# A last block stored from fp32, a last load in halves, and two gate pairs in one row-tiled session: a fused attention and gated-FFN kernel on one core

## Chip, cores and metric

The kernel runs on one core of one Trainium2 chip. The metric is the device time in microseconds. Before the change it was 753.76 us, the median of 6 runs (749.32 to 759.1).

## What is computed

x has 4 batches of 12416 tokens with 128 channels; 32 inducing points I (32x128) are shared by the batches. Two attention steps make new tokens, and a gated FFN of width 1536 follows:

```python
h    = softmax(I @ x.T / sqrt(128)) @ x        # per batch: 32 x 128
y    = softmax(x @ h.T / sqrt(128)) @ h        # per batch: 12416 x 128
gate = sigmoid(y @ w_gate)
out  = (gate * (y @ w_val)) @ w_out            # 49664 x 128, fp32
```

Since y is a mixture of the 32 rows of h, the kernel never forms it: y @ w_gate is the 32-column attention matrix times h @ w_gate. The sigmoid is half of (1 + tanh(half the argument)); the half is applied when the output is evicted.

## The kernel before, in words

**Tiles.** 12288 tokens of a batch are six "quads" of 2048 (QT), and 128 tokens are left as a tail. A block is 512 tokens; 96 blocks cover the quads, and the last one, number 96, is "mixed": the four tails of 128 tokens together. The 1536 columns of the FFN are 12 chunks j of 128. A gate pair p is the chunks 2p and 2p+1.

**Head (lines 81 to 569).** GpSimd issues the six loads of batch 0's quads (`load_x`, L83, with a cast to fp16) and then the loads of the three weights (L116 to L120). For each quad s, TensorE transposes it in two halves of eight 128x128 tiles (`xT_pe`, L476; ScalarE copies half 0 out of PSUM, VectorE half 1), computes 16 scores (`s1n`, L506, with an exp on ScalarE), and accumulates h (`h_mm`, L193). The loop of L515 staggers them: scores of quad s-1, transposes of s, h of s-2. Then h is normalised, multiplied with the weights (`hw_mm`, L242), and `hw_pad` (L256) has GpSimd copy some chunks of it into `pads`, tiles of 128 rows that are zero elsewhere.

**Fills (L351).** The 32 rows of h @ w for a chunk lie in one of four row groups of 32: gates in groups 0 and 1, values in 2 and 3; `rep` holds the attention matrix four times, once for each group. A fill is one matmul of 512 columns with the 32 rows of one group (a row-tiled fill), or, for chunks that have a padded copy (PADG, PADV, L133), with all 128 rows. Before the change PADG is (2, 5): gate pairs 2 and 5 are filled with 128 rows. PADV is (2, 5, 8, 11): one value chunk in each step.

**Main loop (L718).** Each block has four steps k. A step, in program order:

1. `v_fill` of two value chunks into the PSUM tile va (one buffer, two banks), row-tiled
2. one gate pair into a tile g (two buffers of two banks), then its tanh on ScalarE (`g_tanh`, L418, writing T)
3. `v_mul` (L432): VectorE makes u = (T + 1) * va
4. c0 output matmuls (`out_mm`, L445) from the queue `ready`
5. `v_fill` of one value chunk into vb (one buffer, one bank), 128 rows
6. at odd k one more gate pair; at k = 2, in 49 of the blocks, a job (`do_extra`, L651: scores, h sums and the like for a later batch or quad)
7. `v_mul` of vb; c1 output matmuls

Items 1 and 2 are the step's row-tiled session. Gates run ahead of the values: at k = 0 pair 3 is filled, at k = 1 pairs 4 (in the session) and 5 (after vb, 128 rows), at k = 2 pair 0 of the next block, at k = 3 its pairs 1 (in the session) and 2 (after vb, 128 rows). (c0, c1) come from PLAN (L712), or PLAN_JOB where the block has a job. All engines run in the order written (`manual_schedule`, L78); each engine's queue is in order.

**Outputs.** A block's 12 output matmuls accumulate [channels x 512 tokens] in the tile acc (one buffer, one bank). `out_store` (L456) then has ScalarE evict it with the factor 0.5 to fp16 (oT), SP issue a DMA transpose to `on` (tokens on partitions), and GpSimd issue the store, which casts to fp32. For the mixed block these are four stores, one for each batch (L473).

Of the kernel before, what the change touches and what calls it, by code (L numbers as in the profile page):

```python
# [9 lines left out]
F32 = mybir.dt.float32  # L10
F16 = mybir.dt.float16
# [5 lines left out]
P = 128  # L17
TOK = 512
QT = 4 * TOK
# [4 lines left out]
def kernel(  # L24
# [41 lines left out]
    def slot_g(name):  # L66
        return ps_g.tile([P, 2 * TOK], F32, tag="g", name=name)
# [15 lines left out]
    def load_x(b, q):  # L83
        t = xqp.tile([P, QT], F16, tag="xq", name=f"xq_{b}_{q}")
        nc.gpsimd.dma_start(  # L85
            t[:], x[b, ds(q * QT, QT)].rearrange("(p j) c -> p (j c)", j=QT // P)
        )
        xqs[(b, q)] = t
# [24 lines left out]
        out=ident[:], in_=ident[:], compare_op=ALU.not_equal, fill=1.0, base=0,  # L113
        pattern=[[-1, P]], channel_multiplier=1,
    )
    for q in range(2, NQ):  # L116
        load_x(0, q)
    nc.gpsimd.dma_start(wg16[:], moe_w_gate.rearrange("c (j f) -> c j f", f=P))
    nc.gpsimd.dma_start(wv16[:], moe_w_val.rearrange("c (j f) -> c j f", f=P))
    nc.gpsimd.dma_start(wo16[:], moe_w_out.rearrange("(j p) c -> p j c", p=P))  # L120
# [9 lines left out]
    hTs = [pers.tile([P, M], F16, tag=f"hT{b}", name=f"hT_{b}") for b in range(B)]  # L130
    hws = [pers.tile([P, NP2, P], F16, tag=f"hw{b}", name=f"hw_{b}") for b in range(B)]

    PADG, PADV = (2, 5), (2, 5, 8, 11)  # L133
    pads = [pers.tile([P, 8, P], F16, tag=f"hwp{b}", name=f"hwp_{b}") for b in range(B)]
    for t_ in pads:
        nc.gpsimd.memset(t_[:], 0.0)

# [38 lines left out]
    def s1n_mm(ps, b, q, lo, hi):  # L176
        for tk in range(lo, hi):
            j, r = tk % 4, tk // 4
            nc.tensor.matmul(
                ps[:, ds((j * 4 + r) * M, M)], xTs[b][:, ds(q * QT + tk * P, P)], indT[:],  # L180
                start=True, stop=True,
            )
# [10 lines left out]
    def h_mm(ps, b, q, first, last, tail, ch=0, cs=P):  # L193
        for j in range(4):
            nc.tensor.matmul(  # L195
                ps[:, cs:cs + P], ones[:, 0:P], a1n[(b, q)][:, j, :],
                start=first and j == 0, stop=last and j == 3,
            )
            if tail and j == 0:
                nc.tensor.matmul(  # L200
                    ps[:, cs:cs + M], ones[:, 0:P], a1n[(b, "t")][:], start=False, stop=False
                )
        for j in range(4):
            for r in range(4):
                nc.tensor.matmul(  # L205
                    ps[r * M:(r + 1) * M, ch:ch + P],
                    a1_chunk(b, q, 4 * r + j),
                    xqs[(b, q)][:, ts(4 * r + j, P)],
                    start=first and j == 0,
                    stop=last and j == 3 and not (tail and r == 0),  # L210
                )
        if tail:
            nc.tensor.matmul(
                ps[0:M, ch:ch + P], a1n[(b, "t")][:], xtail[:, b, :], start=False, stop=last,
            )
# [40 lines left out]
    def hw_pad(b):  # L256
        for i, p in enumerate(PADG):
            for jj in range(2):
                rows = slice(jj * M, (jj + 1) * M)
                nc.gpsimd.tensor_copy(out=pads[b][rows, 2 * i + jj, :], in_=hws[b][rows, p, :])  # L260
        for i, j in enumerate(PADV):
            g = 2 + j % 2
            rows = slice(g * M, (g + 1) * M)
            nc.gpsimd.tensor_copy(out=pads[b][rows, 4 + i, :], in_=hws[b][rows, j // 2, :])

# [80 lines left out]
    blocks.append(dict(T=B * P, mixed=True))  # L348
    NBK = len(blocks)

    def fill(ps, col, bi, j, val):  # L351
        k = blocks[bi]
        g = (j % 2) + (2 if val else 0)
        if val and j in PADV:
            pad = 4 + PADV.index(j)
        elif not val and j // 2 in PADG:
            pad = 2 * PADG.index(j // 2) + j % 2
        else:
            pad = None
        rows = slice(0, P) if pad is not None else slice(g * M, (g + 1) * M)  # L360

        def weights(b):
            return pads[b][:, pad, :] if pad is not None else hws[b][rows, j // 2, :]

        if not k["mixed"]:
            rep = reps[(k["b"], k["d"])]
            nc.tensor.matmul(  # L367
                ps[:, ds(col, TOK)], weights(k["b"]), rep[rows, 4 * k["i"] + k["r"]],
                start=True, stop=True,
            )  # L370
        else:
            rep = reps["m"]
            for b in range(B):
                nc.tensor.matmul(
                    ps[:, ds(col + b * P, P)], weights(b), rep[rows, b, :],
                    start=True, stop=True,
                )
# [31 lines left out]

    Ts = {}  # L410

    def g_fill(bi, p):
        ps = slot_g(f"g_{bi}_{p}")
        for jj in range(2):
            fill(ps, jj * TOK, bi, 2 * p + jj, False)
        return ps

    def g_tanh(bi, p, ps):  # L418
# [25 lines left out]

    def out_mm(bi, j, u):  # L445
        T = blocks[bi]["T"]
        if bi not in accs:
            accs[bi] = slot_o(f"acc_{bi}")
            done_out[bi] = 0
        c = done_out[bi]  # L450
        nc.tensor.matmul(  # L451
            accs[bi][:, 0:T], wo16[:, j, :], u, start=(c == 0), stop=(c == NJ - 1)
        )
        done_out[bi] = c + 1

    def out_store(bi):  # L456
        k = blocks[bi]
        T = k["T"]
        nch = T // P
        oT = outp.tile([P, TOK], F16, tag="oT", name=f"oT_{bi}")  # L460
        nc.scalar.activation(out=oT[:, 0:T], in_=accs[bi][:, 0:T], func=AF.Copy, scale=0.5)  # L461
        on = outp.tile([P, 4, C], F16, tag="on", name=f"on_{bi}")
        nc.sync.dma_start(on[:, 0:nch, :], oT[:, 0:T], transpose=True)
        if not k["mixed"]:
            row0 = k["b"] * N + (2 * k["d"] + k["i"]) * QT
            nc.gpsimd.dma_start(  # L466
                out[ds(row0, QT)].rearrange("(p j) c -> p j c", j=QT // P)[
                    :, 4 * k["r"]:4 * k["r"] + 4, :],
                on[:],
            )  # L470
        else:
            for b in range(B):
                nc.gpsimd.dma_start(out[ds(b * N + NT0, P)], on[:, b, :])  # L473


    def xT_pe(b, q):  # L476
        for half in range(2):
            ps = slot_g(f"xt_{b}_{q}_{half}")
            v = ps[:].bitcast(F16)
            for j in range(8):  # L480
                nc.tensor.transpose(  # L481
                    v[:, ts(j, P)], xqs[(b, q)][:, ts(8 * half + j, P)], ident[:]
                )
            dst = xTs[b][:, ds(q * QT + half * 8 * P, 8 * P)]
            if half:
                nc.vector.tensor_copy(out=dst, in_=v[:, 0:8 * P])  # L486
            else:
                nc.scalar.copy(out=dst, in_=v[:, 0:8 * P])

    ps = slot_a("warm")  # L490
    warm(ps, 16)
# [11 lines left out]
    s1t_exp(0, ps)  # L503

    hps = slot_a("h_0")
    def s1n(q):  # L506
        an = ep.tile([P, 4, P], F16, tag="a1q", bufs=3, name=f"a1q_0_{q}")
        ps = (slot_o if q % 2 else slot_b)(f"s1n_0_{q}")
        s1n_mm(ps, 0, q, 0, 16)
        nc.scalar.activation(  # L510
            out=an[:].rearrange("p j f -> p (j f)"), in_=ps[:, 0:TOK], func=AF.Exp, scale=SCALE,
        )
        a1n[(0, q)] = an

    for s in range(NQ):  # L515
        if s >= 1:
            s1n(s - 1)
        xT_pe(0, s)
        if s >= 2:
            h_mm(hps, 0, s - 2, s == 2, False, s == 2, TOK, 0)  # L520
    s1n(NQ - 1)
    h_mm(hps, 0, NQ - 2, False, False, False, TOK, 0)
    h_mm(hps, 0, NQ - 1, False, True, False, TOK, 0)
    psd = slot_g("warm2")
    warm(psd, 1)
# [165 lines left out]
    gdone = 0  # L691
    gwant = LEADP

    def g_next():
        nonlocal gdone
        bi, p = divmod(gdone, NP2)
        gp = g_fill(bi, p)
        g_tanh(bi, p, gp)
        gdone += 1

# [8 lines left out]

    PLAN = ((2, 3), (1, 2), (1, 2), (1, 2))  # L712
    PLAN_JOB = ((2, 3), (1, 2), (1, 1), (1, 2))

    g_next()
    g_next()
# [1 line left out]
    for n in range(NBK):  # L718
        for k in range(4):
            for f in ev.get((n, k), ()):  # L720
                f()
            c0, c1 = (PLAN_JOB if n in extra else PLAN)[k]
            gwant = min(NG, gwant + 1)
            ps = slot_a(f"va_{n}_{k}")
            v_fill(ps, n, 3 * k, 2)
            if gdone < gwant:
                g_next()
            ua = v_mul(ps, n, 3 * k, 2)
            ready.extend(prev)
            outs(c0)  # L730
            ps = slot_b(f"vb_{n}_{k}")
            v_fill(ps, n, 3 * k + 2, 1)
            if k % 2:
                gwant = min(NG, gwant + 1)
            post = None
            if k == 2 and n in extra:
                post = do_extra(*extra[n])
            elif gdone < gwant:
                g_next()
            ub = v_mul(ps, n, 3 * k + 2, 1)  # L740
            if post:
                post()
            outs(c1)
            prev = ua + ub
# [34 lines left out]
```

## Time and profile before

| what | value |
|---|---|
| median of 6 runs | 753.76 us |
| profiled execution, its own time | 750.49 us |
| its span | 748.7 us |
| granted TensorE clock, mean | 0.993 |
| ACT T<-g, 582 tanhs of 128x1024 | 568.6 us busy, mean 1023 ns |
| DVE u<-T,va, 388 of 128x1024 | 472.9 us busy, mean 1219 ns |
| DVE u<-T,vb, 388 of 128x512 | 263.6 us busy, mean 679 ns |
| PE acc<-u,wo, 1164 matmuls | 380.9 us busy, mean 382 ns |
| PE g<-rep,hwp, 384 matmuls (128 rows) | 113.8 us busy, mean 377 ns |
| PE g<-rep,hw, 768 matmuls (32 rows) | 148.8 us busy, mean 384 ns |
| wait PE va <- DVE u | 51.3 us, 154 times |
| wait ACT T <- PE g | 49.1 us, 84 times |

A row of the profile's groups reads: line, engine, operation, out<-in, shapes, count; then busy time and the mean of one; then the idle time of the engine just before. A row of the timeline reads: start, duration, engine, line, operation, count, and in brackets how long the engine had idled and what released it. PE is the matmul, PEld the weight load. A matmul's duration is its latency: two of 512 columns on the same rows start about 0.21 us apart, though each shows 0.38. SPq, POOLq are the queues of those engines.

### The profile page before, as it was taken

The numbers are of one execution on the slowest core, as the hardware profiler recorded it, in microseconds if no ns is written. First come the engines' busy times: TensorE is split into PE (matmuls) and PEld (weight loads), VectorE is DVE, ScalarE is ACT, GpSimd is POOL, SyncE is SP. The second block draws the span as 40 slices with busy tenths as digits, with TensorE's granted clock in tenths as the row PEclk, the third lists the DMA queues.
The fourth block names the chain that finished last, engine by engine and source line by source line (L and its number), as shares of the span: only waits on it lengthen the run. The fifth ranks groups of instructions, "written<-read, shape, count | busy, mean of one in ns | idle before, by whom it ended". The sixth has DMA issues, their size and how long they took to land.

```text
span 748.7 us, 12241 instructions
## 1 busy us (share of the span) xinstructions
PE 667.0 (89%) x4525; PEld 250.0 (33%) x4525; DVE 708.3 (95%) x838; ACT 652.5 (87%) x725; POOL 215.0 (29%) x328
## 2 busy tenths in 40 slices
PE   7888999989889889989889899999888888888884
PEld 4433333333333333333333333333333333333332
DVE  2599999999999999999999999999999999999994
ACT  4699999899899989889989989989989989989883
POOL 5236214304413412402611601521530430330001
PEclk9999999999999999999999999999999999999998
DMA  9578994523558997523347899442352352252222
GB/s 179 81 108 151 214 190 96 113 49 72 106 94 157 145 177 155 115 57 78 80 99 139 118 200 180 102 89 56 69 115 51 71 120 57 70 108 60 59 49 57
DMA packets 182300, 80.25 MB, mean 107 GB/s; under 512 B 165952, under 2 KB 166624, under 8 KB 182240
## 3 DMA queue, kind: packets, MB, share of 16 engines
q1 hardware_dynamic: 162112, 40.18, 31.8%
q0 software_dynamic: 20128, 39.30, 24.5%
q8 instruction: 35, 0.57, 0.3%
q14 instruction: 25, 0.20, 0.1%
HBM read 27.80 MB, written 25.43 MB: 71 GB/s over the span
## 4 chain that ended last, share of the span: by engine, by line
DVE 33%; PE 32%; ACT 24%; DMA 6%; issue 3%; POOL 1%; SPq 0%; POOLq 0%; DVEq 0%; ACTq 0%
DVE u L435 31%; ACT T L422 17%; PE acc L451 12%; PE va L367 9%; PE g L367 6%; ACT oT L461 3%; PE vb L367 3%; DMA xT<-xq 3%; DMA xq<-in_x_dram 2%; ACT e L281 1%; ACT e L164 1%; DMA on<-oT 1%; DVE hacc L221 1%; PE h L205 1%; PE h L195 0%
## 5 line engine op out<-in xcount | busy, mean ns | idle before, releaser
L422 ACT ACTIVATE T<-g 128x1024 f16<-128x1024 f32 x582 | 568.6, 1023 | 61.3 <-PE g L367 49.1
L435 DVE SCALAR_TENSOR_TENSOR u<-T,va 128x1024 f16<-128x1024 f16 x388 | 472.9, 1219 | 8.8 <-issue 3.6
L451 PE MATMUL acc<-u,wo 128*128 128x512 f16 x1164 | 380.9, 382 | 5.3 <-DVE u L435 0.4
L435 DVE SCALAR_TENSOR_TENSOR u<-T,vb 128x512 f16<-128x512 f16 x388 | 263.6, 679 | 0.0
L367 PE MATMUL va<-rep,hw 32*128 32x512 f16 x768 | 149.5, 381 | 54.1 <-DVE u L435 51.3
L466 POOL DMA_DIRECT2D out_dram<-on x96 | 52.8, 550 | 478.4 <-DMA on<-oT 469.5
L451 PEld LDWEIGHTS <-wo 128*128 128x128 f16 x1164 | 104.6, 97 | 173.3 <-issue 99.0
L367 PE MATMUL g<-rep,hw 32*128 32x512 f16 x768 | 148.8, 384 | 0.3 <-ACT T L422 0.2
L367 PE MATMUL vb<-rep,hwp 128*128 128x512 f16 x384 | 144.9, 377 | 0.0
L367 PEld LDWEIGHTS <-hw 32*128 32x128 f16 x1536 | 55.5, 91 | 205.1 <-issue 202.5
L367 PE MATMUL g<-rep,hwp 128*128 128x512 f16 x384 | 113.8, 377 | 2.7 <-DVE hT L240 1.8
L367 PEld LDWEIGHTS <-hwp 128*128 128x128 f16 x768 | 74.2, 97 | 71.5 <-issue 25.1
L321 POOL TENSOR_TENSOR a<-e2n,rc 128x512 f16<-128x512 f16 x88 | 89.3, 1042 | 6.1 <-DVE rc L311 5.8
L461 ACT ACTIVATE oT<-acc 128x512 f16<-128x512 f32 x97 | 58.5, 603 | 6.7 <-PE acc L451 3.9
L303 POOL TENSOR_TENSOR tree<-tree 128x256 f32<-128x256 f32 (+2 forms) x33 | 16.2, 491 | 2.6
L303 POOL TENSOR_TENSOR tree<-e2n 128x512 f32<-128x512 f16 x11 | 12.6, 1148 | 11.5 <-DMA e2n<-e 11.5
L486 DVE COPY xT<-xt 128x1024 f16<-128x1024 f16 x6 | 4.2, 692 | 11.6 <-PE xt L481 11.6
L85 POOL DMA_DIRECT2D xq<-in_x_dram x24 | 13.6, 568 | 0.8 <-POOLq L763 0.8
L164 ACT ACTIVATE e<-s 128x1024 f16<-128x1024 f32 x9 | 9.2, 1024 | 3.9 <-PE s L656 3.9
L281 ACT ACTIVATE e<-s 128x1024 f16<-128x1024 f32 x11 | 11.3, 1024 | 0.0
L656 PE MATMUL s<-xT,indT 128*32 128x512 f16 x72 | 6.3, 386 | 3.5 <-DMA xT<-xq 3.5
L260 POOL COPY hwp<-hw 32x128 f16<-32x128 f16 x16 | 4.6, 289 | 16.0 <-ACT hw L253 15.4
(89 smaller groups left out, 159.7 us busy)
## 6 DMA issues: line engine op xcount, KB each, us to landing
out_dram<-on POOLq DMA_DIRECT2D x96, 256.0 KB, 2.7
xq<-in_x_dram POOLq DMA_DIRECT2D x24, 512.0 KB, 6.3
on<-oT SPq DMA_TRANSPOSE x97, 2.4
wg<-in_moe_w_gate_dram POOLq DMA_DIRECT2D x1, 384.0 KB, 16.4
wv<-in_moe_w_val_dram POOLq DMA_DIRECT2D x1, 384.0 KB, 17.8
wo<-in_moe_w_out_dram POOLq DMA_DIRECT2D x1, 384.0 KB, 18.8
rep<-a SPq DMA_TRANSPOSE x22, 4.3
xT<-xq SPq DMA_TRANSPOSE x18, 5.4
```

The costliest lines, as they stand in the source:

```text
L85: nc.gpsimd.dma_start(t[:], x[b, ds(q * QT, QT)].rearrange("(p j) c -> p (j c)", j=QT // P))
L164: nc.scalar.activation(out=e1[:, 0:w], in_=ps[:, 0:w], func=AF.Exp, scale=SCALE)
L205: nc.tensor.matmul(ps[r * M:(r + 1) * M, ch:ch + P], a1_chunk(b, q, 4 * r + j), xqs[(b, q)][:, ts(4 * r + j, P)], start=first and j == 0, ...
L281: nc.scalar.activation(out=e2[:], in_=ps[:], func=AF.Exp, scale=SCALE)
L303: nc.gpsimd.tensor_tensor(out=nxt, in0=cur[:, :, 0:w], in1=cur[:, :, w:2 * w], op=ALU.add)
L321: nc.gpsimd.tensor_tensor(out=a2[:, r], in0=e2n[:, i, :, r, :].unsqueeze(2).to_broadcast((P, 4, 4, M)), in1=rc[:, i, :, r].unsqueeze(2).un ...
L367: nc.tensor.matmul(ps[:, ds(col, TOK)], weights(k["b"]), rep[rows, 4 * k["i"] + k["r"]], start=True, stop=True,)
L422: nc.scalar.activation(out=Ts[bi][:, 2 * p:2 * p + 2, 0:T], in_=ps[:].rearrange("p (a t) -> p a t", a=2)[:, :, 0:T], func=AF.Tanh, scale=0.5,)
L435: nc.vector.scalar_tensor_tensor(out=u[:, :, 0:T], in0=Ts[bi][:, j0:j0 + n, 0:T], scalar=1.0, in1=ps[:].rearrange("p (a t) -> p a t", t=TO ...
L451: nc.tensor.matmul(accs[bi][:, 0:T], wo16[:, j, :], u, start=(c == 0), stop=(c == NJ - 1))
L461: nc.scalar.activation(out=oT[:, 0:T], in_=accs[bi][:, 0:T], func=AF.Copy, scale=0.5)
L466: nc.gpsimd.dma_start(out[ds(row0, QT)].rearrange("(p j) c -> p j c", j=QT // P)[:, 4 * k["r"]:4 * k["r"] + 4, :], on[:],)
```

## The change

- Batch 0's last quad is loaded by two DMAs of 8 tokens a partition each; its transposes, scores and exps are done in halves. In the loop's last turn h of quad 3 stands between the transposes of half 0 and half 1; scores of half 0, h of quad 4, scores of half 1, h of quad 5 follow. With halves, `s1n` writes its exp with a four-dimensional pattern.
- PADG is (2,). Pair 5 is always row-tiled. Pair 2 uses its padded weights only where it is filled after vb (`whole`, at k = 3). `pads` shrinks from 8 to 6 chunks, and `hw_pad` copies two chunks fewer.
- At k = 1 both gate pairs, 4 and 5, are filled in the session, one after the other, ahead of vb; nothing is filled after vb there.
- PLAN goes from ((2,3),(1,2),(1,2),(1,2)) to ((2,2),(0,3),(1,2),(1,2)), PLAN_JOB alike: at k = 1 no output stands ahead of vb, three behind it.
- The mixed block's outputs are made with tokens on partitions: u is the stationary operand (four pieces of 128 tokens), w_out the moving one, 48 matmuls of 128 columns for 12 of 512. Two ScalarE evictions of 128x256 to fp32 replace the one to fp16; four stores follow without a transpose, two issued by SP and two by ScalarE.

```diff
-    for q in range(2, NQ):
+    for q in range(2, NQ - 1):
         load_x(0, q)
+    for half in range(2):
+        nc.gpsimd.dma_start(
+            xl[:, ts(half, QT // 2)],
+            x[0, ds((NQ - 1) * QT, QT)].rearrange("(p j) c -> p (j c)", j=QT // P)[
+                :, ts(half, QT // 2)],
+        )
...
-    PADG, PADV = (2, 5), (2, 5, 8, 11)
+    PADG, PADV = (2,), (2, 5, 8, 11)
...
-        elif not val and j // 2 in PADG:
+        elif not val and whole:
...
     def out_mm(bi, j, u):
+        if bi == NBK - 1:
...
+            for b in range(B):
+                nc.tensor.matmul(
+                    accs[bi][:, ts(b, P)], u[:, ts(b, P)], wo16[:, j, :],
+                    start=(c == 0 and b == 0), stop=(c == NJ - 1), skip_group_check=True,
+                )
...
     def out_store(bi):
+        if k["mixed"]:
+            o32 = outp.tile([P, B, C], F32, tag="o32", bufs=1, name="o32")
+            for h in range(0, B, 2):
+                w = min(2, B - h)
+                nc.scalar.activation(
+                    out=o32[:, h:h + w, :].rearrange("p b c -> p (b c)"),
+                    in_=accs[bi][:, ds(h * P, w * P)], func=AF.Copy, scale=0.5,
+                )
+                for b in range(h, h + w):
+                    eng = nc.sync if b % 2 == 0 else nc.scalar
+                    eng.dma_start(out[ds(b * N + NT0, P)], o32[:, b, :])
+            return
...
     for s in range(NQ):
         if s >= 1:
             s1n(s - 1)
-        xT_pe(0, s)
-        if s >= 2:
+        xT_pe(0, s, 0)
+        if s == NQ - 1:
             h_mm(hps, 0, s - 2, s == 2, False, s == 2, TOK, 0)
-    s1n(NQ - 1)
+        xT_pe(0, s, 1)
+        if 2 <= s < NQ - 1:
+            h_mm(hps, 0, s - 2, s == 2, False, s == 2, TOK, 0)
+    s1n(NQ - 1, ((0, 8),))
     h_mm(hps, 0, NQ - 2, False, False, False, TOK, 0)
+    s1n(NQ - 1, ((8, 16),))
     h_mm(hps, 0, NQ - 1, False, True, False, TOK, 0)
...
-    PLAN = ((2, 3), (1, 2), (1, 2), (1, 2))
-    PLAN_JOB = ((2, 3), (1, 2), (1, 1), (1, 2))
+    PLAN = ((2, 2), (0, 3), (1, 2), (1, 2))
+    PLAN_JOB = ((2, 2), (0, 3), (1, 1), (1, 2))
...
-            gwant = min(NG, gwant + 1)
+            pairs = 2 if k == 1 else 1
+            gwant = min(NG, gwant + pairs)
             ps = slot_a(f"va_{n}_{k}")
             v_fill(ps, n, 3 * k, 2)
-            if gdone < gwant:
+            for _ in range(min(pairs, gwant - gdone)):
                 g_next()
             ua = v_mul(ps, n, 3 * k, 2)
             ready.extend(prev)
             outs(c0)
             ps = slot_b(f"vb_{n}_{k}")
             v_fill(ps, n, 3 * k + 2, 1)
-            if k % 2:
+            if k == 3:
                 gwant = min(NG, gwant + 1)
             post = None
             if k == 2 and n in extra:
                 post = do_extra(*extra[n])
             elif gdone < gwant:
-                g_next()
+                g_next(k == 3)
```

## The prediction

> **What bounds the kernel now.** I read the page first (busy times, chain of waits, groups), then the list of waits, then the timeline of single blocks, of the first 40 us and of the last 30. The page:
>
> ```profile
> PE 667.0 (89%) x4525; PEld 250.0 (33%) x4525; DVE 708.3 (95%) x838; ACT 652.5 (87%) x725; POOL 215.0 (29%) x328
> DVE 33%; PE 32%; ACT 24%; DMA 6%; issue 3%; POOL 1%; SPq 0%; POOLq 0%; DVEq 0%; ACTq 0%
> L435 DVE SCALAR_TENSOR_TENSOR u<-T,va 128x1024 f16<-128x1024 f16 x388 | 472.9, 1219 | 8.8 <-issue 3.6
> ```
>
> VectorE is busy 95% of the span, and its main line idles 8.8 us in all. But its instructions overlap, so I take the start times of its 776 products u from the timeline instead. From a va product to the vb product is always 1.14 us. From a vb product to the next va product the least is 0.62 us: a step cannot go below 1.76 us, a block below 7.04. What lies above 0.62, over blocks 1 to 95, is by step k: 0.4 us (k=0), 6.8 us (k=1), 15.3 us (k=2, where the jobs are), 2.9 us (k=3). At k=1 the gap is 0.63 in 48 blocks and 0.74 to 0.76 in 47. The second kind, in the timeline of block 32 (PE, ACT and DVE rows only):
>
> ```profile
> 266.37 0.60 ACT L461 ACTIVATE oT<-acc 128x512 f16<-128x512 f32 x1
> ...
> 266.52 0.39 PE L367 MATMUL va<-rep,hw 32*128 32x512 f16 x2 [0.19 <-DVE u L435]
> 266.53 0.39 PE L367 MATMUL g<-rep,hw 32*128 32x512 f16 x2
> ...
> 267.01 1.22 DVE L435 SCALAR_TENSOR_TENSOR u<-T,va 128x1024 f16<-128x1024 f16 x1
> 267.02 0.38 PE L451 MATMUL acc<-u,wo 128*128 128x512 f16 x1
> ...
> 267.24 0.38 PE L367 MATMUL vb<-rep,hwp 128*128 128x512 f16 x1
> 267.45 0.59 PE L367 MATMUL g<-rep,hwp 128*128 128x512 f16 x2
> ...
> 267.88 0.59 PE L451 MATMUL acc<-u,wo 128*128 128x512 f16 x2
> 268.14 0.68 DVE L435 SCALAR_TENSOR_TENSOR u<-T,vb 128x512 f16<-128x512 f16 x1
> 268.41 0.39 PE L367 MATMUL va<-rep,hw 32*128 32x512 f16 x2
> ...
> 268.90 1.22 DVE L435 SCALAR_TENSOR_TENSOR u<-T,va 128x1024 f16<-128x1024 f16 x1
> ```
>
> The first output matmul of the block cannot start until ScalarE has emptied the one acc bank (oT ends 266.97). PE is in order, so vb, the padded gate pair and two outputs queue behind it, and the next va fill comes at 268.41, although VectorE had left the va bank at 268.23. In a block of the other kind oT ends at 726.25, the same acc starts 0.38 after the va fill (here 0.50), and the next va fill comes 1.77 after its predecessor (here 1.89). The 47 late blocks are those that follow a block with a job: the job's plan (1,1) leaves one output over, so the twelfth output, and oT after it, come one matmul later. So at k=1 of every second block PE's queue, not VectorE, sets the pace.
>
> The end of the kernel:
>
> ```profile
> 738.28 0.68 DVE L435 SCALAR_TENSOR_TENSOR u<-T,vb 128x512 f16<-128x512 f16 x1
> 738.42 0.97 PE L451 MATMUL acc<-u,wo 128*128 128x512 f16 x3 [0.37 <-DVE u L435]
> ...
> 739.43 0.60 ACT L461 ACTIVATE oT<-acc 128x512 f16<-128x512 f32 x1 [3.88 <-PE acc L451]
> 742.98 2.11 POOL L473 DMA_DIRECT2D out_dram<-on  x4 [6.14 <-DMA on<-oT]
> ```
>
> After the last product the span goes on for 9.7 us, most of it a DMA transpose (issued 740.05, landed 742.45) and four stores issued one by one by GpSimd.
>
> **What the Trainium skill says.** "TensorE: Matmul & The Clock Gate", section "The mechanism": matmuls in different row groups run together, but start and end in program order. The trace agrees: va and g at 266.52 and 266.53. The two gate pairs and va filled together at the loop's start stand at 28.89, 29.03 and 29.12, so a second pair on the same rows costs 0.23 us. "TensorEngine Tiling (Array Packing)", "Key Properties": changing the tiling mode drains the array. The trace shows acc 0.32 after a row-tiled start that occupies about 0.21, so 0.1 us a change; the change adds none. "DMA: Bandwidth & Descriptors", "Rules for kernel authors": spreading DMAs over engines saves only issue time. For 64 KB the issue list agrees: 1.8 us to landing from SP (xt) and from GpSimd (out) alike.
>
> **The change, part by part**, on the profiled execution's clock (span 748.7, its own time 750.49; the median shown is 753.76, 3.3 above it).
>
> *Step k=1, two pairs in one session.* Removed: two full-height matmuls (0.215 each) after vb. Added: two row-tiled ones ahead of it (0.23). Moved: the first output, from ahead of vb to behind it. From the va fill: vb at 0.32 + 0.23 = 0.55, three outputs from 0.76 to 1.41, next va possible at 1.51. VectorE frees va at 0.49 + 1.22 + 0.07 = 1.78, so it sets the pace and the gap is 0.62. The outputs begin at 0.76, past oT's end (0.45 in the late blocks). The new wait: p5 needs the g bank that p3's tanh frees, and vb and the outputs queue behind p5. In blocks 1 to 96 that tanh ends 0.03 to 0.97 us before the va fill, so p5 doesn't wait. PE saves about 0.2 us in 97 blocks, 20 us, but nearly all is hidden by VectorE; worth is the 6.8 us. ScalarE gains in the same late blocks (p5's tanh started 1.57 after the va fill, otherwise 1.44), so its chain does not take it back. Some returns where a job waits for a DMA transpose (PE s <- DMA xT: 3.5 us, 4 times): +0.4. Bounds for this part: 0 (another queue ends the wait) to -8.5 (part of k=3's 2.9 goes too).
>
> *Block 0* is ScalarE-bound: tanhs run back to back from 29.32. p5 (before at 33.15, behind vb at 32.78) now stands ahead of vb, which comes at about 33.47; the next va fill at 34.4 instead of 34.10. +0.3. GpSimd's shorter padding work (two copies of 0.33 and 0.2 a memset less) brings rep earlier, where PE waited 0.25 at 34.44; I count nothing.
>
> *Plan (2,2),(0,3)*: a block still has 13 places for 12 outputs, 12 with a job. Nothing beyond the move above.
>
> *Last quad in halves.* The DMA's landing times in the trace: q4 17.83, q5 19.67. PE reaches q5 at 20.82, because it was held by q4. So q5 is not late here, and halves bring nothing. The new order puts h(3), 0.73 us, between the halves' transposes: the second half's copy on VectorE moves from 22.30 to about 22.9, ending 23.6; its scores follow h(4) at 23.9; exp (0.39, between 0.28 for 128 columns and 0.50 for 384) ends at 24.8; h(5) at 24.83 instead of 24.23: +0.6. If q4 lands 1.4 earlier in an execution (2.46 a quad, as q1 to q3), q5 is late and halves save up to 1. Range -1 to +0.8. The extra issue (0.55) delays the weight loads' issue; GpSimd's wait for a landing before wo (0.58) moves to wv, and wo waits for q1 at 9.02. wo's turn in the queue comes after wv at 23.4, and its use is at 32.5: hidden.
>
> *Last block.* 48 matmuls of 128 columns with their own weight loads replace 12 of 512: 16 such pairs took 1.05 us in the transposes, 0.066 each, 0.26 for four against 0.215; block 96 has no gate fills, so this is hidden but for the last u. Then: last u ready 738.96, four pairs to 739.43; ScalarE 128x256 (0.39) to 739.86; its DMA issue (no row shows ScalarE issuing; SP's took 0.40; between 0.05 and 1) to 740.28; second half to 740.69; the last two stores issued 740.71 (SP's queue is empty since 734.6; ScalarE's second half queues behind its own issue, as counted), landed +1.8 at 742.5, before 746.35. Gone are the transpose (2.4), the wait to 742.98 and three serial issues (1.6). The end: 2.35 us lie behind the landing now, since GpSimd's closing drain lasts to 747.94, while SP's own waits ended at 746.64. With GpSimd idle since 738.8 I take 0.29 + 0.78 behind the landing: end 743.6, **-5.1** (-3.8 if the drain stays; -2.8 if the ScalarE issue also costs 1).
>
> Sum: -6.8 + 0.4 + 0.3 + 0.6 - 5.1 = **-10.6 us**: span 738.1, the profiled execution 739.9, the median 743.2.
>
> **Rivals.** *The loop gives nothing:* k=1's excess reappears at k=2 or k=3, since ScalarE is 87% busy and the blocks with an exp job are bound by it. Against: ScalarE needs 6 x 0.97 + 0.60 = 6.4 us a block of 7.07. Then -10.6 + 6.4 = -4.2: 749.6. *Slower:* p5 waits for p3's tanh at k=1. vb and outputs have 0.27 of slack (1.78 - 1.51), and p5 starts 0.22 after va anyway, so it costs from the point where that tanh ends 0.4 us after the va fill; it ends at least 0.03 before it. An end at +0.6 would cost 0.2 in 97 blocks, 19 us less the tail: 758 and more. It would need ScalarE 0.6 later in every block. *More:* q5 late in the usual execution (head -1 instead of +0.6), k=3 shortened by 1.7: -14, 739.8. *The second pair runs apart from the first* (0.43 instead of 0.23): next va possible at 1.71, still under 1.78, no change.
>
> **Numbers.** Forecast 0.65 (own range 740 to 747), loop gives nothing 0.20, more 0.10, slower 0.05. Range 738 to 751: it leaves out the slow case and the tails. A measurement of this kernel tells about 1% (7.5 us) from no change: faster takes nearly all of the forecast and the larger gain, 0.71; same 0.24; slower 0.05.
>
> **What would show it.** The gap after k=1 at 0.62 to 0.63 in all blocks; p5's g fill directly behind p4's; oT's end before the first acc; last product to end about 4.6 us, no transpose in it; h(5) some 0.6 later against q5's transposes. Wrong if PE's g waits for ScalarE's T show up at k=1, if the gap of k=3 grows by what k=1 lost, or if the end is still 8 us long.

## Result and the profile after

The changed kernel takes 746.34 us, the median of 28 runs (741.66 to 754.24). The kernel before, run beside it, takes 752.57 us, the median of 63 (749.07 to 760.26). The ratio is 0.9915, with a 95% interval from 0.9896 to 0.9935: 6.2 us less, where 10.6 were forecast (743.2, range 738 to 751). The gain, 0.85% by the ratio, is less than the 1% that the forecast gave a chance of 0.71 to pass. The profiled execution of the changed kernel (own time 753.05, span 751.3) is one of its long ones: 10 of the 28 took 741.7 to 744.1, 10 took 748.7 to 754.2, so a run of median length must have lost less than it did.

The page of the changed kernel, its busy times, its chain and its main line:

```profile
PE 660.1 (88%) x4561; PEld 241.6 (32%) x4561; DVE 705.6 (94%) x838; ACT 647.0 (86%) x727; POOL 210.0 (28%) x317
DVE 60%; PE 26%; DMA 5%; ACT 5%; issue 3%; SPq 1%; POOL 0%; ACTq 0%; DVEq 0%; POOLq 0%
L443 DVE SCALAR_TENSOR_TENSOR u<-T,va 128x1024 f16<-128x1024 f16 x388 | 472.9, 1219 | 15.1 <-PE g L375 5.7
```

VectorE's share of the chain went from 33% to 60%: where PE and ScalarE used to pace the steps, VectorE does now. But its main line idles 15.1 us, not 8.8, so something holds it elsewhere. Block 32, which the prediction showed before the change, in the timeline of the changed kernel:

```profile
275.64 0.60 ACT L492 ACTIVATE oT<-acc 128x512 f16<-128x512 f32 x1
...
275.79 0.39 PE L375 MATMUL va<-rep,hw 32*128 32x512 f16 x2 [0.19 <-DVE u L443]
...
275.80 0.60 PE L375 MATMUL g<-rep,hw 32*128 32x512 f16 x4
...
276.28 1.22 DVE L443 SCALAR_TENSOR_TENSOR u<-T,va 128x1024 f16<-128x1024 f16 x1
...
276.39 0.38 PE L375 MATMUL vb<-rep,hwp 128*128 128x512 f16 x1
...
276.60 0.81 PE L472 MATMUL acc<-u,wo 128*128 128x512 f16 x3
...
277.42 0.68 DVE L443 SCALAR_TENSOR_TENSOR u<-T,vb 128x512 f16<-128x512 f16 x1
277.55 0.39 PE L375 MATMUL va<-rep,hw 32*128 32x512 f16 x2
...
278.04 1.22 DVE L443 SCALAR_TENSOR_TENSOR u<-T,va 128x1024 f16<-128x1024 f16 x1
```

Two gate pairs (four fills, 0.60 in one row) stand between va and vb, the outputs start at 276.60, after oT's end at 276.24, and the next va product follows the vb product by 0.62. The end, in the same view:

```profile
745.56 0.68 DVE L443 SCALAR_TENSOR_TENSOR u<-T,vb 128x512 f16<-128x512 f16 x1
...
745.70 0.99 PE L462 MATMUL acc<-wo,u 128*128 128x128 f16 x12 [0.36 <-DVE u L443]
746.73 0.38 ACT L483 ACTIVATE o<-acc 128x256 f32<-128x256 f32 x1 [3.89 <-PE acc L462]
747.14 1.18 SPq L489 DMA_DIRECT2D out_dram<-o  x2
747.14 0.38 ACTq L489 DMA_DIRECT2D out_dram<-o  x1
747.57 0.38 ACT L483 ACTIVATE o<-acc 128x256 f32<-128x256 f32 x1 [0.46 <-ACT o L483]
747.99 0.37 ACTq L489 DMA_DIRECT2D out_dram<-o  x1
```

No transpose and no wait for one: the last store is issued 1.75 after the last product's end (746.24).

To see where the time went, I split each profiled span as the prediction did, by the start times of the 776 products: the first product; block 0 (from its first product to block 1's); what blocks 1 to 95 spend above 0.62 between a vb product and the next va product, by step; and from the last product's end to the end of the span. What these leave is 674.8 to 675.9 us in every kernel, so the columns account for the spans. (e12 and e13 bring several edits together, told below.)

| kernel (all in us) | first product | block 0 | k=1 | k=2 and 3 | end | span |
|---|---|---|---|---|---|---|
| before | 30.4 | 8.66 | 6.8 | 18.2 | 9.8 | 748.7 |
| after | 30.7 | 10.83 | 0.1 | 29.6 | 5.0 | 751.3 |
| e1: loop alone | 29.1 | 10.83 | 0.1 | 30.1 | 10.0 | 755.4 |
| e2: last block alone | 28.9 | 8.62 | 6.9 | 18.1 | 5.1 | 742.5 |
| e3: plan alone | 29.0 | 10.01 | 21.6 | 17.3 | 9.7 | 762.9 |
| e4: block 0 one pair | 29.9 | 9.79 | 0.1 | 19.8 | 5.0 | 739.5 |
| e5: load not halved | 29.1 | 10.83 | 0.1 | 32.6 | 5.2 | 752.7 |
| e6: earlier transposes | 30.9 | 8.95 | 0.1 | 25.7 | 4.7 | 746.1 |
| e7: the same on before | 29.2 | 8.62 | 6.9 | 21.2 | 9.8 | 751.5 |
| e10: block 0 as before | 30.4 | 8.62 | 0.1 | 22.1 | 5.0 | 741.1 |
| e11: old plan | 29.7 | 10.06 | 0.1 | 22.3 | 5.0 | 742.2 |
| e12: e10 and e5 | 29.0 | 8.62 | 0.1 | 26.1 | 5.1 | 743.9 |
| e13: e12, some earlier | 29.3 | 8.62 | 0.1 | 20.9 | 4.8 | 738.7 |
| e14: dummies in block 0 | 30.8 | 9.87 | 0.1 | 22.6 | 5.0 | 743.7 |

From before to after: +0.3, +2.2, -6.7, +11.4, -4.7 is +2.5, against 2.6 between the spans. The two gains are all there. Three columns gave time back in this execution, k=2 and 3 above all.

### The profile page after: what moved, and what is told of

Read it like the earlier page. It is cut to its first block, busy times and chain, and to the rows that moved or that the text cites. A ratio compares the mean times of both kernels' runs of the same rounds, so it can differ in the third digit from the quotient of the medians.

```text
span 751.3 us, 12305 instructions
## 1 busy us (share of the span) xinstructions
PE 660.1 (88%) x4561; PEld 241.6 (32%) x4561; DVE 705.6 (94%) x838; ACT 647.0 (86%) x727; POOL 210.0 (28%) x317
## 4 chain that ended last, share of the span: by engine, by line
DVE 60%; PE 26%; DMA 5%; ACT 5%; issue 3%; SPq 1%; POOL 0%; ACTq 0%; DVEq 0%; POOLq 0%
DVE u L443 59%; PE va L375 13%; PE acc L472 5%; ACT T L430 4%; DMA xT<-xq 4%; PE g L375 2%; DMA xq<-in_x_dram 2%; PE vb L375 2%; PE h L213 1%; PE h L203 1%; PE s L282 1%; PE s L691 1%; DVE rc L319 0%; SPq L294 0%; PE xt L507 0%
## 5 line engine op out<-in xcount | busy, mean ns | idle before, releaser
L430 ACT ACTIVATE T<-g 128x1024 f16<-128x1024 f32 x582 | 561.2, 1024 | 65.7 <-PE g L375 56.9
L443 DVE SCALAR_TENSOR_TENSOR u<-T,va 128x1024 f16<-128x1024 f16 x388 | 472.9, 1219 | 15.1 <-PE g L375 5.7
L472 PE MATMUL acc<-u,wo 128*128 128x512 f16 x1152 | 364.2, 384 | 0.0
L375 PE MATMUL g<-rep,hw 32*128 32x512 f16 x962 | 171.6, 386 | 1.6 <-ACT T L430 1.6
L375 PEld LDWEIGHTS <-hw 32*128 32x128 f16 x1730 | 64.9, 91 | 218.4 <-issue 204.7
L375 PEld LDWEIGHTS <-hwp 128*128 128x128 f16 x574 | 56.1, 98 | 84.6 <-issue 62.3
L375 PE MATMUL g<-rep,hwp 128*128 128x512 f16 x190 | 57.5, 384 | 1.8 <-DVE hT L248 1.8
L172 ACT ACTIVATE e<-s 128x1024 f16<-128x1024 f32 x9 | 9.2, 1023 | 11.8 <-PE s L691 11.7
L411 POOL TENSOR_TENSOR a2q_q<-e2q_q,rcq_q 128x512 f16<-128x512 f16 x7 | 7.1, 1039 | 8.4 <-DVE rcq_q L406 8.3
```

The costliest lines, as they stand in the source:

```text
L172: nc.scalar.activation(out=e1[:, 0:w], in_=ps[:, 0:w], func=AF.Exp, scale=SCALE)
L375: nc.tensor.matmul(ps[:, ds(col, TOK)], weights(k["b"]), rep[rows, 4 * k["i"] + k["r"]], start=True, stop=True,)
L430: nc.scalar.activation(out=Ts[bi][:, 2 * p:2 * p + 2, 0:T], in_=ps[:].rearrange("p (a t) -> p a t", a=2)[:, :, 0:T], func=AF.Tanh, scale=0.5,)
L443: nc.vector.scalar_tensor_tensor(out=u[:, :, 0:T], in0=Ts[bi][:, j0:j0 + n, 0:T], scalar=1.0, in1=ps[:].rearrange("p (a t) -> p a t", t=TO ...
L472: nc.tensor.matmul(accs[bi][:, 0:T], wo16[:, j, :], u, start=(c == 0), stop=(c == NJ - 1))
```

## Experiments

**e1, the loop alone.** The kernel before with the loop's edits only: PADG, two pairs at k=1, the new plan.

```diff
-    PADG, PADV = (2, 5), (2, 5, 8, 11)
+    PADG, PADV = (2,), (2, 5, 8, 11)
...
+            pairs = 2 if k == 1 else 1
+            gwant = min(NG, gwant + pairs)
...
-    PLAN = ((2, 3), (1, 2), (1, 2), (1, 2))
+    PLAN = ((2, 2), (0, 3), (1, 2), (1, 2))
```

> The kernel before with the loop part alone: pair 5 row-tiled behind pair 4 at k=1, PADG (2,), and the new output plan; head and last block as before. Theory S (the forecast's shortfall lies in the loop: block 0 stalls with TensorE's clock lowered, and waits for xT transposes take some of the k=1 gain back): gap after k=1 at 0.62 in all blocks (-6.7 us), block 0 about 2 us longer, so -2 to -5 us. Rival (the shortfall lies in head and tail): -6 us or more, block 0 unchanged.

Measured: 749.47 us (746.12 to 759.43), ratio 0.9976 [0.9953, 0.9999]: -2.2 us by the medians (-0.1 to -3.5 by the interval), where the loop's terms in the forecast (-6.8 + 0.4 + 0.3) come to -6.1. In the profiled execution, a long one (757.18), k=1 lost its 6.7 us, block 0 grew by 2.2, and k=2 and 3 grew by 12.

**e2, the last block alone.** The kernel before with `out_mm` and `out_store` of the changed one.

```diff
     def out_store(bi):
+        if k["mixed"]:
...
+                    eng = nc.sync if b % 2 == 0 else nc.scalar
+                    eng.dma_start(out[ds(b * N + NT0, P)], o32[:, b, :])
+            return
```

> The kernel before with the last block's part alone (tokens on partitions, four fp32 stores by SP and ScalarE). Theory S: last product to end about 5.0 us instead of 9.7, so -4.7 us and nothing else changed. Rival: the tail gives under 3 us by the clock and the rest is noise of the profile.

Measured: 746.41 us (744.29 to 749.11), 0.9923 [0.9901, 0.9946], -5.2 us. The last block's share is as forecast; so of the 4.4 us by which the forecast missed, about 3.9 are missing in the loop.

**e3, the plan alone.** The kernel before with the new PLAN and PLAN_JOB, one pair in the session as before.

```diff
-    PLAN = ((2, 3), (1, 2), (1, 2), (1, 2))
+    PLAN = ((2, 2), (0, 3), (1, 2), (1, 2))
```

> The kernel before with only PLAN and PLAN_JOB changed: pair 5 stays padded and behind vb. Theory S1 (what held k=1 was the output standing ahead of vb and waiting for oT): from the va fill vb at 0.32, pair 5 to 0.96, three outputs to 1.61, next va possible at 1.71, before VectorE frees it at 1.78: the gap after k=1 is 0.62 to 0.63 in all blocks as in the whole change, without block 0's stall, -5 to -7 us. Rival S2 (the gain needs the shorter gate pair): the gap stays at 0.7 or more in the blocks after a job, and the time within 2 us of before.

Measured: 763.89 us (763.55 to 764.68), 1.0153 [1.0134, 1.0172]: +12 us. The gap after k=1 is 0.85 in 92 of 95 blocks. A step k=1 of e3 in its timeline:

```profile
264.28 0.68 DVE L435 SCALAR_TENSOR_TENSOR u<-T,vb 128x512 f16<-128x512 f16 x1
264.42 0.39 PE L367 MATMUL va<-rep,hw 32*128 32x512 f16 x2 [0.41 <-DVE u L435]
...
264.42 0.39 PE L367 MATMUL g<-rep,hw 32*128 32x512 f16 x2
...
265.01 0.38 PE L367 MATMUL vb<-rep,hwp 128*128 128x512 f16 x1 [0.20 <-DVE u L435]
...
265.23 0.59 PE L367 MATMUL g<-rep,hwp 128*128 128x512 f16 x2
...
265.66 0.81 PE L451 MATMUL acc<-u,wo 128*128 128x512 f16 x3
266.04 0.68 DVE L435 SCALAR_TENSOR_TENSOR u<-T,vb 128x512 f16<-128x512 f16 x1
...
266.40 0.39 PE L367 MATMUL va<-rep,hw 32*128 32x512 f16 x2
```

And its list of waits (engine, tile and line, what it waited for: us in all, times, the longest):

```profile
PE vb L367 <- DVE u L435: 19.0, 95, 0.2
```

Neither theory allowed for that. With nothing ahead of it, vb is not early: it waits 0.20 in 95 blocks until VectorE's previous vb product (264.28 to 264.96) has left vb's only bank, and starts 0.59 after the va fill. The prediction did not have this wait. It puts a hole before vb into every step k=1. The old plan put an output there, which in the late blocks waited for oT; the changed kernel puts the second gate pair there; the plan alone leaves it empty and lets two gate fills and three outputs stand between vb and the next va fill, which comes 1.98 after its predecessor instead of 1.76.

**e4, one pair in block 0.** The changed kernel; in block 0 pair 5 goes back behind vb, the plan stays new.

```diff
-            pairs = 2 if k == 1 else 1
+            pairs = 2 if k == 1 and n else 1
...
-            if k == 3:
+            if k == 3 or (k == 1 and n == 0):
```

> The whole change, but block 0 fills pair 5 behind vb (row-tiled); all other blocks as in the change. Theory S: block 0's four steps take 8.7 us again instead of 10.8, the clock stays at full, and the time is about 2 us under the whole change, near 744. Rival (block 0's loss is an accident of one execution): block 0 no shorter or the time unchanged at 746.

Measured: 742.89 us (740.38 to 753.37), 0.9900 [0.9873, 0.9926]. The profiled one, 739.5, has what the loop should give: -0.5 (first product), +1.1 (block 0), -6.7, +1.6 and -4.7 make -9.2, which is the difference of the spans. But 8 of its 21 runs took 747.9 and more, and block 0, at 9.79, did not come back to the 8.7 of the theory; nor did its clock stay full (0.88 over 30 to 44 us).

**e10, block 0 wholly as before.** e4, with block 0's padded fills of pairs 2 and 5 and its old plan as well.

```diff
-    PADG, PADV = (2,), (2, 5, 8, 11)
+    PADG, PADV = (2, 5), (2, 5, 8, 11)
...
+            if n == 0:
+                c0, c1 = ((2, 3), (1, 2), (1, 1), (1, 2))[k]
+            pairs = 2 if k == 1 and n else 1
...
-                g_next()
+                g_next(n == 0)
```

> The whole change, with block 0 as it was before (pairs 2 and 5 on 128 rows, pair 5 behind vb, old plan); blocks 1 to 96 as in the change. Theory C (in block 0 ScalarE is the bound, row-tiled pairs make TensorE busy for less of the time, its clock is lowered to half for some 5 us, and that is what block 0 loses): clock 1.0 from 28 to 40 us, block 0's steps 8.7 us in all, time 2 us under the change in executions of the same kind. Rival (the order of pair 5 alone, which the variant with pair 5 row-tiled behind vb already undid): no better than that variant's block 0, 9.8 us.

Measured: 743.25 us (740.67 to 744.42), 0.9867 [0.983, 0.9903]. Block 0 is back at 8.62, with the clock at 1.00 from 30 us on, and no run is longer than 744.42. The interval still overlaps that of the changed kernel.

**e14, dummy matmuls in block 0.** The changed kernel; in block 0, at k=0 and 1, three matmuls on ones go ahead of each gate pair of the session, nine in all.

```diff
+            early = slot_b(f"vb_{n}_{k}") if n == 0 and k < 2 else None
             for _ in range(min(pairs, gwant - gdone)):
+                if early is not None:
+                    warm(early, 3)
                 g_next()
```

> The whole change, plus nine matmuls on ones in block 0 (three ahead of each gate pair at k=0 and k=1, into the bank of vb before vb is filled; they compute nothing that is used). They keep TensorE busy while it waits for ScalarE. Theory C (the lowered clock makes most of block 0's loss, the place of pair 5 the lesser part): clock 1.0 from 32 to 40 us, block 0's steps 9.2 to 9.8 us instead of 10.8, and the slow executions of 748 to 754 become rare. Rival (the place of pair 5 makes the loss): block 0 stays at 10.5 us or more with the clock at 1.0.

Measured: 744.05 us (742.29 to 751.18), 0.9919 [0.9877, 0.996]; block 0 at 9.87. The granted clock of its block 0 is 1.00 (the column after POOL's count):

```profile
32.00:36.00 4.00, 3.79 (x22) 1.18 (x19) 2.51 (x4) 3.54 (x4) 1.52 (x2) 1.00 0.47 94
```

Yet only about half of block 0's loss is gone, since the nine matmuls hold up PE themselves: pair 5's fill starts 3.69 after the first product, against 2.77 in e6, whose block 0 has no dummies and the full clock too. Two of the seven runs still took 750.1 and 751.2, so the long runs did not become rare.

**e5, the load not halved.** The changed kernel with the head of the one before.

```diff
-    for q in range(2, NQ - 1):
+    for q in range(2, NQ):
         load_x(0, q)
...
-    s1n(NQ - 1, ((0, 8),))
-    h_mm(hps, 0, NQ - 2, False, False, False, TOK, 0)
-    s1n(NQ - 1, ((8, 16),))
+    s1n(NQ - 1)
+    h_mm(hps, 0, NQ - 2, False, False, False, TOK, 0)
```

> The whole change without the last quad's halves (loads, transposes, scores and exps of batch 0 as before). Theory H (halves cost, as PE reaches the last quad after its data): the time from q4's landing to the first product is 0.6 to 0.9 us shorter (about 11.6 instead of 12.5 us), all else equal. Rival: halves save, as the last quad's data are what PE waits for: 0.5 us longer.

Measured: 748.33 us (741.62 to 754.49), 0.9894 [0.9834, 0.9955]. The interval holds that of the changed kernel, so the time decides nothing here. Its first product is at 29.06, against 30.66, but the clock of the two heads differs (see "Head" below).

**e6 and e7, earlier transposes.** The DMA transposes of x for batches 1 to 3 are put two steps earlier in SP's queue (e6 on the changed kernel, e7 on the one before).

```diff
-                ((1, 0), (2, 0), (2, 2), (3, 2), 4, (5, 2), (7, 9)),
-                ((5, 0), (6, 0), (6, 2), (7, 2), 8, (9, 2), (12, 13)),
-                ((8, 0), (9, 0), (9, 3), (10, 2), 11, (12, 2), (14, 15)),
+                ((1, 0), (2, 0), (2, 0), (3, 0), 4, (5, 2), (7, 9)),
+                ((5, 0), (6, 0), (6, 0), (7, 0), 8, (9, 2), (12, 13)),
+                ((8, 0), (9, 0), (9, 1), (10, 0), 11, (12, 2), (14, 15)),
```

> The whole change, with the DMA transposes of the next batch's quads issued two steps (half a block) earlier in SP's queue. Theory W (the times between 746 and 754 of the change are executions in which score jobs wait for these transposes, TensorE's clock falls in the wait and the next step pays again): the waits of s for xT drop from 10 us to under 2, the mean clock is 0.99 or more in every execution, times lie within 3 us of each other around 741. Rival (the spread has another cause, or earlier transposes collide with other DMA work): median and spread as in the change, 746, 742 to 754.

> The kernel before with the same earlier transposes. Theory W: the same waits are smaller here (3.5 us in the profile shown), so it gains 2 to 4 us: about 748 to 749 with a narrower spread; against this kernel the whole change with earlier transposes then gains 7 to 9 us. Rival: no change, 751.6.

Measured: e6 747.84 us (745.39 to 748.77), 0.9931 [0.9907, 0.9954]; e7 754.89 (753.31 to 758.15), 1.0041 [1.0024, 1.0058]. Neither gained; e7 is 3.5 us slower than the kernel before. In both, the gap after k=2 of block 4 is the longest of all: 5.9, against 4.8 in the changed kernel and 1.1 in the one before. It is not a wait for xT, for which e6's score job stood only 0.85. VectorE and GpSimd held the step:

```profile
64.87 1.30 SPq L294 DMA_TRANSPOSE e2n<-e  x1
...
68.24 1.14 POOL L311 TENSOR_TENSOR tree<-e2n 128x512 f32<-128x512 f16 x1 [0.43 <-DMA e2n<-e]
...
71.43 0.35 DVE L319 RECIPROCAL rc<-rs 128x32 f32<-128x32 f32 x1 [4.98 <-POOL rs L311]
```

The reciprocal stands ahead of the va product in VectorE's queue, and waited 4.98 for GpSimd's sum (rs). That sum began when the transpose of the exps (e2n) had landed, and SP issued this transpose 25.0 after block 1's first product, against 19.4 in the kernel before: it stands in SP's one queue behind the moved transposes of x, the first of which took 5.91 to issue. Spreads are narrow (3.4 and 4.8 us).

**e11, two pairs with the old plan.** The changed kernel with PLAN and PLAN_JOB of the one before.

```diff
-    PLAN = ((2, 2), (0, 3), (1, 2), (1, 2))
-    PLAN_JOB = ((2, 2), (0, 3), (1, 1), (1, 2))
+    PLAN = ((2, 3), (1, 2), (1, 2), (1, 2))
+    PLAN_JOB = ((2, 3), (1, 2), (1, 1), (1, 2))
```

> The whole change with the old output plan: at k=1 one output stands between the two gate pairs and vb again. Theory P1 (two pairs make TensorE's queue short enough by themselves): from the va fill the output starts at 0.54 at the latest, vb at 0.76, two outputs to 1.41, so the gap after k=1 stays 0.62 to 0.63 in all blocks and the time is the change's. Rival P2 (moving the output is what frees k=1): the gap after k=1 returns to 0.7 and more in the blocks after a job, +5 us.

Measured: 746.1 us (743.41 to 749.05), 0.9919 [0.9889, 0.9948], as the changed kernel. The gap after k=1 is 0.62 to 0.63 in all 95 blocks: the place of pair 5 does it, the plan adds nothing.

**e12 and e13, what the runs point to.** e12 is e10 with the old head (e5's edit). e13 is e12 with e6's earlier transposes, for batches 2 and 3 only.

```diff
+            if b == 0:
+                plan = (
+                    ((1, 0), (2, 0), (2, 2), (3, 2), 4, (5, 2), (7, 9)),
...
+            else:
+                plan = (
+                    ((1, 0), (2, 0), (2, 0), (3, 0), 4, (5, 2), (7, 9)),
...
```

> The change's loop and tail, with the head as before (no halves) and block 0 as before (padded pairs 2 and 5, pair 5 behind vb, old plan). Theory: head and block 0 each cost the change something, and the lowered clock in block 0 also leads to the long xT waits at blocks 4 and 8; without both: first product near 29.1, block 0 8.7 us, waits at blocks 4 and 8 under 3 us, 739 to 742 with no executions above 747. Rival (long waits come at random, whatever block 0 does): executions of 748 to 753 remain as in the change, median near 745.

> The variant before, with the transposes of batches 2 and 3 (not batch 1) half a block earlier. Theory: earlier transposes hurt only in blocks 2 to 8, where DMA is saturated, and save 1 to 2.5 us in later blocks, as both earlier runs showed at blocks 32, 52 and 56: about 738 to 740. Rival: no difference from the variant before.

Measured: e12 744.97 us (741.44 to 746.66), 0.9895 [0.9856, 0.9935], longer than the 739 to 742 of its theory; e13 739.58 us (738.02 to 744.35), 0.9843 [0.9806, 0.988], the best of all, 11.8 us under the kernel before by the ratio, and the only one whose interval lies wholly under that of the changed kernel. Not all of e13's lead over e12 is its edit: in blocks 4 and 8, where both are the same, e13's gaps are 2.6 us shorter in the profiled executions; in blocks 32, 52 and 56, which the edit touches, the sum of the gaps is 0.9 shorter (2.56, 1.62, 1.65 against 1.36, 0.86, 2.67).

## Why the prediction was right or wrong

**k=1: right in size (-6.8 forecast, -6.7 measured), half right in mechanism.** The late blocks did wait for PE's queue behind oT, and the gap is now 0.62 in 90 blocks and at most 0.64. But vb's early start, "vb at 0.32 + 0.23 = 0.55", rested on the queue alone. e3 shows that its bank holds vb until 0.59 even with nothing ahead of it (0.60 in block 32 above); the second pair came out free because it fills this hole. The prediction's outputs "from 0.76" came at 0.81, still inside the slack. "The loop gives nothing" falls: k=2 and 3 did grow, but not because ScalarE took the step's gain back. They grew at a few jobs (below), and in e4 by only 1.6 us. The slower rival, p5 waiting for p3's tanh, occurs in block 0 and nowhere else.

**Plan: "nothing beyond the move above" holds** (e11). By itself it costs 12 us (e3).

**Last block: -5.1 forecast, -4.7 measured** (9.76 to 5.04; e2 -5.2 in time). Up to the landing it went as worked out: last stores issued 1.75 after the last product, as forecast; ScalarE's DMA issue 0.37 to 0.38 (0.40 taken), 128x256 in 0.38 (0.39), landed after 1.8 at 749.8. The missing 0.4 is the end behind the landing: 1.5, not 1.07. SP's last waits ended 0.72 after the landing, where 0.29 was taken. That GpSimd's drain would not hold the end was right: 2.35 lay behind the landing before.

**Head: +0.6 forecast, +0.4 to +0.7 measured at equal clock.** The first product is at 29.7 to 30.9 in the six kernels with the halves (mean 30.4), and at 28.9 to 30.4 in the eight without (mean 29.25). But this difference of 1.1 mixes two clocks. The head of the changed kernel, then that of e4, which has the halves too:

```profile
20.00:24.00 4.00, 3.97 (x88) 3.26 (x88) 0.69 (x1) 1.99 (x3) 0.00 (x0) 0.72 1.37 193
...
20.00:24.00 4.00, 3.44 (x92) 2.73 (x88) 0.69 (x1) 2.27 (x4) 0.00 (x0) 1.00 1.37 196
```

The clock was 0.72 to 0.84 there in four profiled executions (before, after, e6 and e14), and 0.65 a little later (24 to 28 us) in e10. Where it was full throughout, the first product is at 29.7 and 29.9 with the halves (e11, e4) and at 28.9 to 29.3 without (seven kernels): about 0.7 later. From the last quad's transposes to its h they need 3.51 with the halves (e4, e10, e11) and 3.03 to 3.12 without. Where it was lowered over 20 to 24 us, the halves start at 30.66 to 30.93, against 30.38 before. So the forecast's size holds, on few executions. By time nothing can be told of it: the intervals of e5 and the changed kernel overlap, and so do those of e12 and e10. Why the clock fell in one head of eight without the halves and in four of six with them stays open.

**Block 0: +0.3 forecast, +0.3 to +2.2 measured.** This step failed. Its working is right where the clock is full: e6, whose block 0 is the changed kernel's own, has 8.95 (+0.3). e6's timeline of block 0:

```profile
33.70 0.39 PE L375 MATMUL g<-rep,hw 32*128 32x512 f16 x2 [0.53 <-ACT T L430]
...
34.02 0.39 PE L375 MATMUL vb<-rep,hwp 128*128 128x512 f16 x1
...
34.45 0.69 DVE L443 SCALAR_TENSOR_TENSOR u<-T,vb 128x512 f16<-128x512 f16 x1 [0.47 <-PE vb L375]
...
34.99 0.39 PE L375 MATMUL va<-rep,hw 32*128 32x512 f16 x2
```

The next va fill comes 4.06 after the first product (30.93), against 3.72 before. The same place in the changed kernel:

```profile
33.43 0.61 PE L375 MATMUL g<-rep,hw 32*128 32x512 f16 x2 [0.31 <-ACT T L430]
...
33.98 0.61 PE L375 MATMUL vb<-rep,hwp 128*128 128x512 f16 x1
...
34.62 0.69 DVE L443 SCALAR_TENSOR_TENSOR u<-T,vb 128x512 f16<-128x512 f16 x1 [0.90 <-PE vb L375]
...
35.80 0.61 PE L375 MATMUL va<-rep,hw 32*128 32x512 f16 x2
```

The same instructions take 0.61 where e6 has 0.39, and the va fill comes 5.14 after the first product. The windows give the reason (the clock is again the column after POOL's count); changed kernel first, then e6:

```profile
core 0: us, PE busy (x) PEld busy (x) DVE busy (x) ACT busy (x) POOL busy (x), PEclk, DMA share, GB/s
...
32.00:36.00 4.00, 3.50 (x14) 0.78 (x13) 2.39 (x3) 3.21 (x4) 1.40 (x2) 0.56 0.49 98
36.00:40.00 4.00, 4.00 (x32) 1.52 (x29) 2.94 (x3) 2.64 (x3) 0.00 (x0) 0.58 0.01 1
```

```profile
32.00:36.00 4.00, 3.29 (x28) 1.14 (x26) 3.17 (x5) 4.00 (x5) 1.66 (x2) 1.00 0.43 86
36.00:40.00 4.00, 3.77 (x33) 1.43 (x29) 3.96 (x7) 3.76 (x5) 0.00 (x0) 1.00 0.06 13
```

TensorE ran at half its clock from 32.5 to 39.3 us, and about 1.9 us of block 0 were lost to that. e1 and e5 have the same 10.83, with 0.76 over 30 to 44 us as in the changed kernel. Before, e2, e7, e10, e12 and e13, whose block 0 is the old one, have 1.00 there and 8.62 to 8.66; e3, e4 and e11, each with a part of the change in block 0, have 0.88 and 9.79 to 10.06. The Trainium skill, "TensorE: Matmul & The Clock Gate", "What's actually happening", has a monitor set the clock by how busy PE has been, over a free-running window, which fits one program with two outcomes. It puts the throttled state after an idle window of about 3.4 us; here there was no such pause (from 30 to 33 us PE was busy for 1.9, and its waits were under 1 us each), and the measurement decides. On the length the trace fits it: the clock stays at half for 6.82 us in the changed kernel, e1 and e5, and for half of that, 3.41, in e3, e4, e11 and in every head where it fell. So the clock fell in six of the seven profiled executions with something changed in block 0 and no dummies, and in none of the six with the old block 0. That the two pairs bring the fall on by giving PE less work is not shown: with e14's dummies the clock stayed at 1.00, but so it did in e6 without them, and e3, whose gate pairs are the old ones, lost clock with the plan alone.

**"+0.4 returned where a job waits for a DMA transpose": right in place, far off in size.** The lists of waits of before and of the changed kernel, in this order:

```profile
PE s L656 <- DMA xT<-xq: 3.5, 4, 1.5
```

```profile
PE s L691 <- DMA xT<-xq: 10.3, 5, 3.7
```

Of the 8.4 us by which k=2 grew, 8.0 lie at three score jobs, blocks 4, 8 and 32: gaps of 4.79, 5.27 and 2.67, against 1.10, 1.36 and 2.25. The gaps behind them, at k=3, are 1.30, 1.45 and 2.09, against 0.63 to 0.70. Why is xT late? The queues of SP and GpSimd in the timeline, before:

```profile
39.93 1.19 SPq L463 DMA_TRANSPOSE on<-oT  x1
40.25 0.61 POOL L85 DMA_DIRECT2D xq<-in_x_dram  x1
46.14 0.54 POOL L466 DMA_DIRECT2D out_dram<-on  x1 [5.28 <-DMA on<-oT]
49.68 0.60 POOL L85 DMA_DIRECT2D xq<-in_x_dram  x1
```

and after:

```profile
42.63 1.19 SPq L494 DMA_TRANSPOSE on<-oT  x1
42.71 0.60 POOL L85 DMA_DIRECT2D xq<-in_x_dram  x1
49.39 0.54 POOL L496 DMA_DIRECT2D out_dram<-on  x1 [6.08 <-DMA on<-oT]
52.92 0.60 POOL L85 DMA_DIRECT2D xq<-in_x_dram  x1
```

Read them from block 1's first product on (39.04 and 41.49). oT of block 0 is later by 0.24, because PE was late, so `on` is issued at 1.14 instead of 0.89, only 0.08 ahead of a 512 KB load where it was 0.32 ahead. It lands 6.2 us after its issue instead of 5.6. GpSimd, in order, waits for it with the store, and issues the second load at 11.4 instead of 10.6. That load lands 2.7 later, and the transpose that reads it, which stands behind others in SP's queue, 3.3 later (28.8 against 25.5), in the middle of block 4's job. A quarter of a microsecond at the start is 3.7 us at the job, passed on by queues that wait in order.

The other traces fit this. In e1 and e5, whose block 0 also takes 10.83, oT of block 0 starts at 0.70 and 0.78 (before: 0.27), the second load lands at 19.5 and 19.6, and block 4's gap is 4.8 and 4.9. In seven kernels where oT comes at 0.27 or 0.28 and `on` lands by 6.9 (before, e2, e4, e10, e11, e13, e14), that load lands at 16.8 to 17.3, and the gap is 0.95 to 2.28. e4 and e11 are among them: their half clock ended 3.0 and 3.2 us before block 1's first product, that of the three late kernels 1.6 to 2.2. (e6 and e7, with moved transposes, are told above.) A late oT is not the only trigger: in e12 and e3 `on` lands at 8.1 although oT is in time, and e12, with the old block 0, then waits 7.8 us for xT in all. What decides that is open.

How often it happens is less clear. With the change's loop and last block, the kernels with the old block 0 (e10, e12, e13) have no run of 18 at 747.2 or more; the others (after, e4, e5, e11, e14) have 25 of 70. But the kernel before has the old block 0 too, and 12 of its 63 runs lie 5.5 us or more above its lowest, which is where 747.2 lies for the changed kernel. So the old block 0 can only make long runs rarer. The mean clock recorded with each run goes along with the time: 0.994 to 0.997 in the changed kernel's ten shortest runs, 0.984 to 0.989 in nine of its ten longest (0.994 in the other). Which of the two is the cause these figures do not tell.

**Sum.** By the medians: last block -5.2 (e2), loop -2.2 (e1), and +1.2 is left for the head; each of these times is uncertain by 1.5 to 1.7 us, so this does not measure the head. The forecast's two large terms stand. What failed is the step that priced block 0 and the jobs by their instruction times, "+0.3" and "+0.4", as if clock and transfers stayed what they were. Where the loads are on time the forecast comes near: e4's profiled span is 9.2 shorter although its block 0 lost 1.1, and 10 of the changed kernel's 28 runs lie within 1.6 us of 743.2. That the median lies in the stated range is partly luck: no rival of the prediction held either loss, so the range was not made for them.

## What to carry to other kernels

Before pricing what stands ahead of an instruction, ask what else could hold it: a bank that the previous product still reads makes a hole, and work put into that hole is free while work taken out of it only leaves it empty. A step that makes the slack engine wait at the start of a long pipeline should be priced twice, with the clock that it had and with half of it, and then followed through the in-order queues to the transfers that land last. Where such a change pays in 95 blocks and hurts in the first, try leaving the first as it was (e10: 743.25 against 746.34 us).

## What was not expected of the hardware

- TensorE's clock fell to 0.5 in block 0 while the profile shows PE busy or waiting under 1 us at a time, and the same block in another kernel kept 1.00 (above). The half clock came in stretches of 3.41 or 6.82 us, in block 0 and in some heads.
- The DMA transpose to `on` landed 5.6 us after its issue when issued 0.32 ahead of a 512 KB load and after 6.2 when 0.08 ahead, against a median of 2.4 in the issue list. In the first case it landed before the load (6.5 and 8.1 us after block 1's first product), in the second after it (7.3 and 6.8).
- A store of 64 KB lands in 1.7 us issued by SP and 1.8 by ScalarE, whose issue took 0.37 to 0.38; the span ended 1.5 after the last landing with GpSimd idle, 2.35 before.
